# Fills of the third and fourth K stack behind a GpSimd copy of the second layer norm's result

## The chip, the cores and the metric

The kernel runs on one core of a Trainium2 chip. The core has five engines with a queue each: TensorE (PE, matrix products and transposes), VectorE (DVE), ScalarE (ACT), GpSimd (POOL) and SyncE (SP), which here issues every DMA. An engine works through its queue in order and waits at an instruction until the semaphores it needs have been raised by other engines. The metric is the time of one execution on the device in microseconds; shown is the median of several runs.

## The reference

The input `x` has 2048 rows of 512 in float32. The computation is one transformer block: a layer norm, an attention with memory, a residual, a second layer norm, a gated feed-forward part (GEGLU, 1376 wide) and a residual. Cut to what matters here:

```python
q, k, v = LN(x) @ wq, LN(x) @ wk, LN(x) @ wv      # 32 heads of 16, in 4 segments of 512 rows
for s in range(4):                                # M, z: a running memory per head
    p = softmax(q[s] @ k[s].T * 0.25 + causal_mask)
    o = g * (phi(q[s]) @ M) / (phi(q[s]) @ z + 1e-6) + (1 - g) * (p @ v[s])
    M, z = M + phi(k[s]).T @ v[s], z + sum(phi(k[s]))      # phi(t) = t + 1 or exp(t)
h = x + concat(o) @ wo
out = h + (gelu(LN(h) @ w_gate) * (LN(h) @ w_up)) @ w_down
```

## The kernel before

**Units and stages.** The 16 units of the attention are pairs of a chunk `c` (8 heads) and a segment `s`; the first is (0, 0), the second (0, 1). A unit has `qkv` (projections), `mem` (reading the memory), and for each of its two halves `Q` of four heads `pass_a` (row maxima of the logits) and `pass_b` (exponentials and the product with V). Then follow the output projection (`wo_seg`), the second layer norm of the block and the feed-forward part. Products are made of three float32r products of high and low parts, so most values exist as a rounded copy (made on ACT, as in L506) and a rest (made on DVE, as in L507, or on POOL, as in L394 and L410).

**The layer norms at the start.** `ln1(0)` and `ln1(1)` normalise the first and the second segment. For each, DVE takes statistics (L450, L451), works out the factors in twelve tiny steps (L455 to L466) and then normalises four tiles of 128x512 in place with four TENSOR_SCALAR instructions (L471). PE transposes them, four transposes for each of four column blocks `dc` (L497); ACT and DVE split every block into high and low parts (`xt`, L506 and L507). The transposes of `ln1(1)` write to PSUM banks of the pool `PD`, which has three banks and is shared with the projections: a bank is given back when its last reader is done, for example the two copies of a v projection's result on ACT (`vaug`, L576) or the DVE step of `phi` (L548). `ln1(2)` takes its statistics on ACT (L436, L445) with the two scratch tiles `junk`, which `pass_a` needs too (L711).

**The K stacks.** Four tiles `stk` hold K in the layout that `pass_a` and `pass_b` multiply with. DMAs write the K rows into them (L615); all else is constant and is filled once: by `c_stk(i, after)`, which for each half of the partitions issues one ACT copy of ones (64 partitions x 1024, L378) and one POOL memset of zeros (L381). So a stack has two ACT and two POOL instructions. Stacks 0 and 1 belong to the first unit, stacks 2 and 3 to the second.

**What sets the order.** No order is written by hand. The whole program is first listed as operations with an engine, a duration guessed in the code, a priority (a lower number goes first) and the values they read and write; `Sched.run` then deals them out greedily. At each step it takes, among the operations that could start within 0.059 us of the earliest possible start, the one with the lowest priority number. The guessed costs that matter here: a POOL copy of one column 0.1 us, the block of twelve small steps and four normalising steps of an early layer norm `3700 / 960 + 0.072` = 3.93 us, and from the end of an operation to the start of one that needs it 0.165 us (DVE to POOL), 0.08 (POOL to ACT), 0.27 (PE to ACT). Priorities: the splits of `ln1(1)` -2.21, the fills of stack 2 -2.2, those of stack 3 -1.2, the `vaug` copies of the first unit -1.58.

The order that comes out is the order of the engines' queues. The waits on the chip are set apart from it, from the tiles that instructions read and write. A value without a tile, such as those handed to `after`, orders the plan alone: nothing on the chip waits for it. That is why `ln1(0)` ends with a real instruction, a POOL copy of one column of its last normalised tile into `tick` (L523): the copy waits on the chip for the norm, and whatever stands behind it in POOL's queue waits with it. Its value `vcalm` orders the early fills behind it in the plan.

Of the kernel before, what the change touches and what calls it, by code (L numbers as in the profile page):

```python
# [212 lines left out]
def infini_geglu(ctx: ExitStack, tc: tile.TileContext, x, wq, wk, wv, wo, beta,  # L213
                 wg, wu, wd, out):
    nc = tc.nc
# [6 lines left out]
    def sb(name, shape, dt=F32):  # L222
        return p0.tile(shape, dt, name=name)
# [10 lines left out]
    def act(n, prio, fn, ins, outs, src=0.067, **k):  # L234
        return S.op("ACT", n / 1200 + src, prio, fn, ins, outs, **k)
# [4 lines left out]
    def pool(dur, prio, fn, ins, outs, **k):  # L240
        return S.op("POOL", dur, prio, fn, ins, outs, **k)

    def dma(prio, fn, ins, outs, lat=2.2, dur=0.58, **k):
        return S.op("SP", dur, prio, fn, ins, outs, lat=lat, **k)
# [61 lines left out]
    tick = sb("tick", [P, 1])  # L306
# [4 lines left out]
    vident, vamask, vmmask, vgt, vg1 = (Val() for _ in range(5))  # L311
# [31 lines left out]
                                base=0, channel_multiplier=1)  # L343
    pool(0.5, -9, c_ident, [], [vident])

    vcalm = Val()

# [1 line left out]
    vone, vq0, vk0, vv0 = Val(), [Val() for _ in stq_t], [Val() for _ in stk_t], [Val() for _ in va_t]  # L351
# [6 lines left out]
    def c_fill():  # L358
        for i, t in enumerate(stq_t):
            pool(0.93, -4.2 + 0.1 * i, lambda t=t: nc.gpsimd.memset(t.bitcast(F32), 0.0),  # L360
                 [vcalm] if i > 1 else [], [vq0[i]])
        for i, t in enumerate(va_t):
            def ones(t=t):
                nc.gpsimd.memset(t[:, :, 16:136:17], 1.0)
                nc.gpsimd.memset(t[:, :, 136:152], 1.0)
            pool(0.25, -3.5 + 0.1 * i, ones, [vcalm], [vv0[i]])

        def c_amask():
            nc.gpsimd.memset(amask, 0.0)
            nc.gpsimd.affine_select(amask[:, 3 * P:], amask[:, 3 * P:], pattern=[[-1, P]],  # L370
                                    compare_op=OP.is_ge, fill=NEG, base=0, channel_multiplier=1)
        pool(1.0, -3, c_amask, [vcalm], [vamask])

    def c_stk(i, after):
        t = stk_t[i]
        for a in range(2):
            own, other = slice(64 * a, 64 * a + 64), slice(64 - 64 * a, 128 - 64 * a)
            act(2 * D, -4.2 + i, lambda a=a, own=own: nc.scalar.activation(  # L378
                t[own, :, a], one[own, :, None].to_broadcast([64, 2, D]), AF.Copy),
                [vone] + after, [vk0[i]], src=0.1, chain=True)  # L380
            pool(0.93, -4.2 + i, lambda a=a, other=other: nc.gpsimd.memset(  # L381
                t[other, :, a].bitcast(F32), 0.0), after, [vk0[i]], chain=True)


    def split_weight(prio, src, pool_, w=D, rows=P, lo="POOL", after=(), early=3.0, dur=0.58):
        r = Val(PRAW)
        v = Val(pool_)
        dma(prio - early, lambda: nc.sync.dma_start(r.t[:rows, :w], src), [], [r], lat=3.0, dur=dur)
        act(w, prio, lambda: nc.scalar.activation(v.t[:rows, 0, :w], r.t[:rows, :w], AF.Copy),  # L389
            [r], [v], src=0.092)  # L390
        r.writers += [q for a in after for q in a.writers]
        sub = dict(op=OP.subtract)
        if lo == "POOL":
            pool(0.14 + 2.13e-3 * w, prio, lambda: nc.gpsimd.tensor_tensor(  # L394
                v.t[:rows, 1, :w], r.t[:rows, :w], v.t[:rows, 0, :w].bitcast(F32), **sub), [r], [v])
        else:
            dve(w, prio, lambda: nc.vector.tensor_tensor(
                v.t[:rows, 1, :w], r.t[:rows, :w], v.t[:rows, 0, :w].bitcast(F32), **sub), [r], [v])
        return v

    def split_wv(h, cp, prio, early, after=(), dur=0.58):
        hi, lo = WV[h, cp] = Val(PWV), Val(PWV)
        for k in range(2):
            r = Val(PRAW)
            dma(prio - early, lambda r=r, k=k: nc.sync.dma_start(
                r.t, wv[cp][:, k * D:(k + 1) * D]), [], [r], lat=3.0, dur=dur)
            act(D, prio, lambda r=r, k=k: nc.scalar.activation(hi.t[:, k], r.t, AF.Copy), [r], [hi],
                src=0.092, chain=True)
            r.writers += [q for a in after for q in a.writers]
            pool(1.23, prio, lambda r=r, k=k: nc.gpsimd.tensor_tensor(  # L410
                lo.t[:, k], r.t, hi.t[:, k].bitcast(F32), op=OP.subtract), [r, hi], [lo],
                chain=True)
# [99 lines left out]
    def ln1(s):  # L512
        prio = 2 * UNIT[0, s] + (-4.21)
        rows = [Val(PROW1 if s < 2 else PROW) for _ in range(4)]
        for t in range(4):
            r0 = (4 * s + t) * P
            dma(prio - 3, lambda t=t, r0=r0: nc.sync.dma_start(rows[t].t, x[r0:r0 + P]), [],
                [rows[t]], lat=2.0, dur=0.85 if s < 2 else 0.58)
        layer_norm(prio, rows, XT[s], off=s > 1, done=[Val()] if s < 2 else [],
                   behind=XT[0] if s == 1 else [], scratch=PPV if s < 2 else None)  # L520
        if s == 0:

            pool(0.1, prio, lambda: nc.gpsimd.tensor_copy(tick, rows[3].t[:, 0:1]), [rows[3]], [vcalm])  # L523


    va0 = list(vv0)
# [2 lines left out]
    W, STQ, STK, PQ, VA, MB, OM, MAXED = {}, {}, {}, {}, {}, {}, {}, {}  # L529
# [122 lines left out]
    def mem(U):  # L652
        c, s = UNITS[U]
        if not s:
            return
        prio = 2 * U + (-0.2)
        om = OM[U] = Val(POM)
        pq, mb = PQ[U], MB[UNIT[c, s - 1]]
        for n in range(2):
            pm, cc = Val(PD), Val(PCC)  # L660

            def f(n=n, pm=pm):
                for t in range(2):
                    nc.tensor.matmul(pm.t[:, 136 * t:136 * t + 136],  # L664
                                     pq.t[:, (2 * n + t) * P:(2 * n + t + 1) * P], mb.t,
                                     start=True, stop=True)
            pe(0.47, prio, f, [pq, mb], [pm], acq=[om, cc])

            def nd(pm):
                return pm.t[:, 0:272].rearrange("p (t j e) -> p t j e", t=2, j=8)  # L670
            dve(16, prio, lambda pm=pm, cc=cc, nd=nd: nc.vector.tensor_scalar(
                nd(pm)[:, :, :, 16], nd(pm)[:, :, :, 16], 1e-6, None, op0=OP.add), [], [pm])
            dve(128, prio, lambda pm=pm, nd=nd: nc.vector.reciprocal(
                nd(pm)[:, :, :, 16], nd(pm)[:, :, :, 16]), [], [pm])
            dve(16, prio, lambda pm=pm, cc=cc, nd=nd: nc.vector.tensor_tensor(
                cc.t, nd(pm)[:, :, :, 16],
                gt[:, None, 8 * c:8 * c + 8].to_broadcast([P, 2, 8]), op=OP.mult), [pm, vgt], [cc])

            def g(n=n, pm=pm, cc=cc, nd=nd):
                o4 = om.t.rearrange("p (t j e) -> p t j e", t=4, j=8)  # L680
                nc.vector.tensor_tensor(o4[:, 2 * n:2 * n + 2], nd(pm)[:, :, :, 0:16],
                                        cc.t[:, :, :, None].to_broadcast([P, 2, 8, 16]),
                                        op=OP.mult)
            dve(256, prio, g, [pm, cc], [om], chain=True)
# [247 lines left out]


    ln1(0)
    c_fill()
    for i in range(2):
        W[0, 0, i] = split_weight(-4 + 0.1 * i, (wq, wk)[i][0], PW, lo="DVE" if i == 0 else "POOL",
                               early=3.05, after=[vcalm], dur=0.85)
    split_wv(0, 0, -3.8, 2.5, [vcalm], 0.85)
    c_stk(0, [])  # L940
    c_stk(1, [vcalm])
    qkv(0)
    ln1(1)

    dma(1, lambda: nc.sync.dma_start(
# [11 lines left out]
    for U in range(16):  # L957
        c, s = UNITS[U]
        if U:
            qkv(U)  # L960
        if U == 0:
            c_stk(2, [VA[0]])
            c_stk(3, [VA[0]])
        if s % 2 and U < 15:
            h, cn = divmod(U // 2 + 1, NCH)
            for i in range(2):
                W[h, cn, i] = split_weight(2 * (U + 1) + (-3.175), (wq, wk)[i][cn], PW)
            if c % 2:
                split_wv(h, cn // 2, 2 * (U + 1) - 2.4, 3.0)
        if U in LN1_AT:  # L970
            ln1(LN1_AT[U])
        mem(U)
        pass_a(2 * U)
        if U:
            pass_b(2 * U - 1)
        pass_a(2 * U + 1)
        pass_b(2 * U)
# [7 lines left out]
    def at(p, f):  # L985
        return 40 + 24 * p + 2 * forder.index(f)
# [133 lines left out]
    for p in range(2):  # L1120
# [8 lines left out]
        for n, f in enumerate(forder):  # L1129
            k = 11 * p + n + 2  # L1130
            if k == 12:
                B[1] = blocks()
                for s in range(2):
                    prio = at(0, 8) + s
                    rows = [Val(PROW) for _ in range(4)]
# [53 lines left out]
```

## Time and profile before

| | |
|---|---|
| median of 3 runs | 850.38 us (849.77 to 851.44) |
| the profiled execution, its own time | 850.29 us |
| its span from first to last instruction | 848.2 us |
| PE busy | 825.0 us, 97% of the span |
| DVE, ACT, POOL busy | 621.8, 511.7, 458.7 us |
| mean granted PE clock | 0.998 of full speed |

A row of the timeline has the start in microseconds from the start of the span, the duration (of the whole group where equal instructions are merged: x4), the engine, the line of the kernel, the operation, the tile written and the tile read, and in brackets how long the engine had been idle and what ended that. SPq rows are DMA issues. In a table by windows, each row is a stretch of time with the busy time of every engine and the granted PE clock. The chain of waits goes back from the last instruction to what released it; its rows have a start, a length and what ran.

### The profile page before, as it was taken

The numbers are of one execution on the slowest core, as the hardware profiler recorded it, in microseconds if no ns is written. First come the engines' busy times: TensorE is split into PE (matmuls) and PEld (weight loads), VectorE is DVE, ScalarE is ACT, GpSimd is POOL, SyncE is SP. The second block draws the span as 40 slices with busy tenths as digits, with TensorE's granted clock in tenths as the row PEclk, the third lists the DMA queues.
The fourth block names the chain that finished last, engine by engine and source line by source line (L and its number), as shares of the span: only waits on it lengthen the run. The fifth ranks groups of instructions, "written<-read, shape, count | busy, mean of one in ns | idle before, by whom it ended". The sixth has DMA issues, their size and how long they took to land.

```text
span 848.2 us, 15681 instructions
## 1 busy us (share of the span) xinstructions
PE 825.0 (97%) x4924; PEld 656.3 (77%) x4924; DVE 621.8 (73%) x1963; ACT 511.7 (60%) x966; POOL 458.7 (54%) x791
## 2 busy tenths in 40 slices
PE   4899999999999999999999999999999999999998
PEld 4787777877788777887777688788888877788886
DVE  7788877779867778868698675565666885756656
ACT  6767667578755666557445763774656764636441
POOL 6433534434335453445333673588878767779650
PEclk9999999999999999999999999999999999999999
DMA  7444432444344333243343464422212351122102
GB/s 248 120 119 96 96 74 69 108 103 96 85 121 122 89 85 97 48 121 90 107 122 122 126 230 143 122 72 63 63 51 62 119 158 38 50 63 62 51 1 100
DMA packets 64179, 82.90 MB, mean 98 GB/s; under 512 B 25056, under 2 KB 27040, under 8 KB 64096
## 3 DMA queue, kind: packets, MB, share of 16 engines
q1 hardware_dynamic: 64096, 81.91, 34.8%
q8 instruction: 39, 0.64, 0.3%
q14 instruction: 44, 0.36, 0.2%
HBM read 43.14 MB, written 12.58 MB: 66 GB/s over the span
## 4 chain that ended last, share of the span: by engine, by line
PE 92%; DVE 4%; ACT 2%; issue 1%; DMA 1%; SPq 0%; POOL 0%; ACTq 0%; DVEq 0%; POOLq 0%
PE bank L1031 24%; PE bank L1092 14%; PE bank L536 10%; PE bank L701 9%; PE bank L756 9%; PE bank L785 8%; PE bank L862 5%; PE bank L565 4%; PE bank L497 2%; PE bank L808 2%; PE bank L664 1%; PE bank L640 1%; PE bank L632 1%; PE bank L855 1%; ACT pt L760 1%
## 5 line engine op out<-in xcount | busy, mean ns | idle before, releaser
L711 DVE CUSTOM_DVE_ANT_0 junk<-bank,amask 128x256 f32<-128x256 f32 (+3 forms) x512 | 231.0, 486 | 54.1 <-PE bank L701 49.8
L764 POOL TENSOR_SCALAR_AFFINE_SELECT pt<-pt 128x128 f32<-128x128 f32 (+1 forms) x448 | 131.8, 314 | 202.5 <-ACT pt L760 192.1
L760 ACT ACTIVATE pt<-bank 128x512 f32<-128x512 f32 x320 | 177.8, 602 | 63.0 <-PE bank L756 50.4
L701 PE MATMUL bank<-stk,stq 128*128 128x512 f32 (+2 forms) x384 | 130.5, 386 | 0.9 <-DVE nm L711 0.5
L756 PE MATMUL bank<-stq,stk 128*128 128x384 f32 (+3 forms) x512 | 119.8, 325 | 1.3 <-ACT pt L760 0.8
L536 PE MATMUL bank<-xt,w 128*128 128x512 f32 x384 | 109.2, 397 | 0.0
L756 PEld LDWEIGHTS bank<-stq,stk 128*128 128x128 f32 x512 | 85.8, 189 | 15.4 <-ACT pt L760 6.2
L1097 DVE TENSOR_TENSOR pt<-pt,bank 128x512 f32<-128x512 f32 x96 | 64.9, 685 | 28.7 <-PE bank L1092 28.3
L701 PEld LDWEIGHTS bank<-stk,stq 128*128 128x128 f32 x384 | 66.8, 189 | 19.5 <-issue 9.3
L536 PEld LDWEIGHTS bank<-xt,w 128*128 128x128 f32 x384 | 70.0, 189 | 10.9
L785 PE MATMUL bank<-pt,vaug 128*32 128x512 f32 (+3 forms) x1024 | 76.0, 436 | 0.0
L785 PEld LDWEIGHTS bank<-pt,vaug 128*32 128x32 f32 x1024 | 28.4, 109 | 39.9 <-issue 31.8
L1001 POOL TENSOR_TENSOR w<-raw,w 128x512 fp32r<-128x512 f32 (+2 forms) x36 | 42.4, 1180 | 25.4 <-ACT w L999 24.1
L394 POOL TENSOR_TENSOR w<-raw,w 128x512 fp32r<-128x512 f32 (+1 forms) x26 | 34.1, 1312 | 40.6 <-ACT w L389 24.0
L1031 PE MATMUL bank<-xt,stk 128*128 128x512 f32 (+1 forms) x189 | 53.0, 394 | 0.3 <-ACT pq L1038 0.3
L565 PE MATMUL bank<-wv,xt 128*128 128x256 f32 x384 | 52.7, 284 | 0.0
L565 PEld LDWEIGHTS bank<-wv,xt 128*128 128x128 f32 x384 | 50.6, 190 | 1.1
L1031 PE MATMUL bank<-xt,w 128*128 128x512 f32 (+1 forms) x183 | 50.8, 391 | 0.0
L1001 POOL TENSOR_TENSOR stk<-raw,stk 128x512 fp32r<-128x512 f32 (+3 forms) x32 | 36.9, 1155 | 20.1 <-ACT stk L999 19.7
L804 ACT ACTIVATE pvs<-bank 128x512 f32<-128x512 f32 x32 | 19.2, 598 | 44.9 <-PE bank L785 44.9
L1031 PE MATMUL bank<-stk,w 128*128 128x512 f32 (+1 forms) x162 | 45.5, 392 | 0.0
L711 DVE DVE_READ_ACCUMULATOR2_ANT nm<- 128x1 f32 x512 | 42.2, 82 | 0.0
(271 smaller groups left out, 1731.3 us busy)
## 6 DMA issues: line engine op xcount, KB each, us to landing
stq<-hl SPq DMA_DIRECT2D x96, 128.0 KB
stk<-hl SPq DMA_DIRECT2D x192, 64.0 KB
row<-x SPq DMA_DIRECT2D x24, 256.0 KB
raw<-wg SPq DMA_DIRECT2D x20, 256.0 KB
raw<-wu SPq DMA_DIRECT2D x20, 256.0 KB
raw<-wd SPq DMA_DIRECT2D x20, 256.0 KB
o_dram<-o SPq DMA_DIRECT2D x32, 128.0 KB
row<-o_dram SPq DMA_DIRECT2D x16, 256.0 KB
```

Source lines behind the costliest of these rows:

```text
L536: nc.tensor.matmul(pm.t, w.t[:, wi, dc * P:(dc + 1) * P], XT[s][dc].t[:, xi, :], start=dc == 0 and n == 0, stop=dc == ND - 1 and n == 2)
L565: nc.tensor.matmul(pm.t[:, 256 * t:256 * t + 256], XT[s][dc].t[:, xi, t0:t0 + P], whl[wi].t[:, h, 256 * (dc % 2):256 * (dc % 2) + 256], st ...
L701: nc.tensor.matmul(sa.t[:, k * w:(k + n) * w].rearrange("x (n w) -> x n w", n=n), sq.t[:, p, i * P:(i + 1) * P], sk.t[:, p, a:a + n, 0:w], ...
L711: nc.vector.tensor_tensor_reduce(out=junk.t[:, :w], in0=sa.t[:, k * w:(k + 1) * w], in1=amask[:, D - w:], op0=OP.add, op1=OP.min, scale=-1 ...
L756: nc.tensor.matmul(sc.t[:, lo:lo + D - q0], sk.t[:, p, a, q0:q0 + P], sq.t[:, p, q0:D], start=True, stop=True)
L760: act(D, prio, lambda: nc.scalar.activation(e.t, sc.t, AF.Exp), [sc], [e])
L764: nc.gpsimd.affine_select(v, v, pattern=pat + [[1, P]], compare_op=OP.is_ge, fill=0.0, base=0, channel_multiplier=-1)
L785: nc.tensor.matmul(pv.t[32 * n:32 * n + 32, kb * P:D], va.t[:, kb, 17 * j:17 * j + 32], e.t[:, lo:lo + D - kb * P], start=kb == 0, stop=la ...
L1001: pool(0.14 + 2.13e-3 * (hi - lo), prio, lambda: nc.gpsimd.tensor_tensor(v.t[:, 1, :hi - lo], r.t[:, lo:hi], v.t[:, 0, :hi - lo].bitcast(F ...
L1031: nc.tensor.matmul(dst.t[:w], v.t[:, wi, c0 + j * w:c0 + (j + 1) * w], b[bk][j].t[:, xi, :], start=first and j == 0 and n == 0, stop=j == ...
L1092: nc.tensor.matmul(pm.t, HH[p, f, s][hi].t[:w, t * P:(t + 1) * P], v.t[:w, wi, :], start=f == fl[0] and n == 0, stop=f == fl[-1] and n == 2)
L1097: dve(D, prio, lambda a=a, pm=pm: nc.vector.tensor_tensor(a.t, a.t, pm.t, op=OP.add), [pm], [a])
```

## The change

`ln1(1)` gets a POOL copy of one column of its last normalised tile too, and `vcalm` becomes a pair of values, one for each of the two layer norms. What hung on `vcalm` hangs on `vcalm[0]` now. The fills of stacks 2 and 3, which were ordered behind `VA[0]` (the `vaug` copies of the first unit), are ordered behind `vcalm[1]`, the new copy.

```diff
-    vcalm = Val()
+    vcalm = [Val(), Val()]
...
-                 [vcalm] if i > 1 else [], [vq0[i]])
+                 [vcalm[0]] if i > 1 else [], [vq0[i]])
...
-        if s == 0:
-
-            pool(0.1, prio, lambda: nc.gpsimd.tensor_copy(tick, rows[3].t[:, 0:1]), [rows[3]], [vcalm])
+        if s < 2:
+
+            pool(0.1, prio, lambda: nc.gpsimd.tensor_copy(tick, rows[3].t[:, 0:1]), [rows[3]],
+                 [vcalm[s]])
...
-    c_stk(1, [vcalm])
+    c_stk(1, [vcalm[0]])
...
         if U == 0:
-            c_stk(2, [VA[0]])
-            c_stk(3, [VA[0]])
+            c_stk(2, [vcalm[1]])
+            c_stk(3, [vcalm[1]])
```

The lines left out put `vcalm[0]` for `vcalm` in the same way, in the fills of `vaug`, in the mask and in the first weights.

More of the change, by code (lines that the diff above doesn't have):

```diff
@@ L365, in ones @@
                 nc.gpsimd.memset(t[:, :, 136:152], 1.0)
-            pool(0.25, -3.5 + 0.1 * i, ones, [vcalm], [vv0[i]])
+            pool(0.25, -3.5 + 0.1 * i, ones, [vcalm[0]], [vv0[i]])
         def c_amask():
@@ L371, in c_amask @@
                                     compare_op=OP.is_ge, fill=NEG, base=0, channel_multiplier=1)
-        pool(1.0, -3, c_amask, [vcalm], [vamask])
+        pool(1.0, -3, c_amask, [vcalm[0]], [vamask])
     def c_stk(i, after):
@@ L937, in infini_geglu @@
         W[0, 0, i] = split_weight(-4 + 0.1 * i, (wq, wk)[i][0], PW, lo="DVE" if i == 0 else "POOL",
-                               early=3.05, after=[vcalm], dur=0.85)
-    split_wv(0, 0, -3.8, 2.5, [vcalm], 0.85)
+                               early=3.05, after=[vcalm[0]], dur=0.85)
+    split_wv(0, 0, -3.8, 2.5, [vcalm[0]], 0.85)
     c_stk(0, [])
-    c_stk(1, [vcalm])
+    c_stk(1, [vcalm[0]])
     qkv(0)
```

## The prediction

> **What bounds the kernel now.** I read the page's totals and its chain first, then the table by windows, then the timeline of each engine around the second layer norm.
>
> ```profile
> span 848.2 us, 15681 instructions
> PE 825.0 (97%) x4924; PEld 656.3 (77%) x4924; DVE 621.8 (73%) x1963; ACT 511.7 (60%) x966; POOL 458.7 (54%) x791
> PE 92%; DVE 4%; ACT 2%; issue 1%; DMA 1%; SPq 0%; POOL 0%; ACTq 0%; DVEq 0%; POOLq 0%
> ```
>
> The chain of waits that ended last runs through PE for 92% of the span. So a change is worth what it takes out of PE's idle time. The windows from 40 us on say where idle time is left:
>
> ```profile
> 450.00:500.00 50.00, 47.13 (x299) 34.46 (x300) 39.09 (x114) 30.41 (x57) 28.62 (x54) 1.00 0.45 148
> 830.00:848.20 18.20, 14.41 (x64) 11.61 (x62) 10.97 (x17) 2.39 (x4) 0.00 (x0) 1.00 0.31 116
> sum 808.20, PE 798.22 PEld 634.00 DVE 591.90 ACT 484.01 POOL 436.60; mean PE 46.95 PEld 37.29 DVE 34.82 ACT 28.47 POOL 25.68
> ```
>
> Behind 40 us PE idles 808.20 - 798.22 = 10.0 us: 18.20 - 14.41 = 3.8 at the very end, 50 - 47.13 = 2.9 where attention passes into the rest of the block, 3.3 in all else. So a head start won before 40 us is kept to the end if the later order of work is as good as it is now. The change acts before 40 us, on DVE and POOL:
>
> ```profile
> 10.03 1.92 DVE L471 TENSOR_SCALAR pt<-pt,mv,ln 128x512 f32<-128x512 f32 x4
> 12.01 0.58 POOL L523 COPY tick<-pt 128x1 f32<-128x1 f32 x1 [5.29 <-DVE pt L471]
> 12.53 1.84 POOL L360 MEMSET stq<- 128x1024 f32 x2
> 13.14 0.69 DVE L507 TENSOR_TENSOR xt<-bank,xt 128x512 fp32r<-128x512 f32 x1 [0.60 <-ACT xt L506]
> 15.70 0.69 DVE L507 TENSOR_TENSOR xt<-bank,xt 128x512 fp32r<-128x512 f32 x1 [0.16 <-ACT xt L506]
> 17.52 0.95 POOL L381 MEMSET stk<- 64x1024 f32 x1
> 20.55 5.91 PE L565 MATMUL bank<-wv,xt 128*128 128x256 f32 x48
> 21.82 2.56 POOL L394 TENSOR_TENSOR w<-raw,w 128x512 fp32r<-128x512 f32 x2
> 22.48 0.15 DVE L455 TENSOR_SCALAR bank<-mv 128x4 f32<-128x4 f32 x1
> 24.44 4.45 POOL L381 MEMSET stk<- 64x1024 f32 x4
> 24.88 4.29 DVE L471 TENSOR_SCALAR pt<-pt,mv,ln 128x512 f32<-128x512 f32 x4
> 29.10 0.67 DVE L548 SCALAR_TENSOR_TENSOR pk<-bank,e 128x512 f32<-128x512 f32 x1
> ```
>
> The four normalising steps of the first norm take 1.92 us, the same four of the second 4.29. Beside the second run the four memsets of stacks 2 and 3: 4.45 us for four, 1.11 each, against 0.95 for one (17.52). Steps and memsets take turns, 4.29 / 4 = 1.07 for a step. So the fills had not waited for `VA[0]` at all; that value orders only the plan.
>
> [...]
>
> What the slow norm holds up:
>
> ```profile
> 28.07 0.33 PE L497 MATMUL bank<-ident,pt 128*128 128x128 f32 x1 [0.84 <-DVE pt L471]
> 29.23 2.56 PE L497 MATMUL bank<-ident,pt 128*128 128x128 f32 x9 [0.84 <-DVE pt L471]
> 29.00:30.00 1.00, 0.65 (x2) 0.36 (x3) 1.00 (x6) 0.26 (x1) 0.00 (x0) 0.50 0.67 156
> 31.00:32.00 1.00, 1.00 (x5) 0.93 (x4) 0.46 (x2) 0.74 (x2) 0.00 (x0) 0.50 0.42 102
> 27.05 1.05 ACT L378 ACTIVATE stk<-one 64x1024 fp32r<-64x1024 f32 x1
> 29.75 0.60 ACT L506 ACTIVATE xt<-bank 128x512 fp32r<-128x512 f32 x1 [1.65 <-PE bank L497]
> 30.98 0.60 ACT L506 ACTIVATE xt<-bank 128x512 fp32r<-128x512 f32 x1 [0.64 <-PE bank L497]
> 31.83 0.60 ACT L506 ACTIVATE xt<-bank 128x512 fp32r<-128x512 f32 x1 [0.26 <-PE bank L497]
> 32.46 1.05 ACT L378 ACTIVATE stk<-one 64x1024 fp32r<-64x1024 f32 x1
> 34.65 2.12 ACT L378 ACTIVATE stk<-one 64x1024 fp32r<-64x1024 f32 x2
> 36.80 0.72 ACT L445 ACTIVATE junk<-row,bn 128x512 f32<-128x512 f32 x1
> 37.76 0.69 DVE L711 CUSTOM_DVE_ANT_0 junk<-bank,amask 128x512 f32<-128x512 f32 x1 [1.48 <-ACT junk L445]
> 33.22 1.65 PE L536 MATMUL bank<-xt,w 128*128 128x512 f32 x6
> 38.51 0.50 PE L701 MATMUL bank<-stk,stq 128*128 128x512 f32 x1 [0.54 <-DVE nm L711]
> ```
>
> PE waits for single normalised tiles at 28.07 and 29.23, and its clock falls to 0.50 in the windows from 29 to 32. ACT waits three times for transposes, then does the rest without a pause: splits, the ACT part of the fills, L445. L445 gives back the scratch tile that DVE's first row maximum needs at 37.76, and PE goes on with `pass_a` at 38.51.
>
> **The change part by part.** *The memsets leave the norm.* The steps start at 24.88 as before, since nothing ahead of them is touched: the weight rests L394 end at 21.82 + 2.56 = 24.38. They take 1.92 instead of 4.29, so they end about 26.80 instead of 29.17: **2.37 us sooner**. DVE's L548 follows at once, and with it the PSUM bank for the next transposes.
>
> *What is late next.* It is ACT. From the fill at 27.05 to L445 its queue holds idle time of 1.65 + 0.64 + 0.26 = 2.55 us; more than that can't go, because the instructions stay the same. So DVE's first maximum and PE's restart at 38.51 come earlier by the lesser of 2.37 and 2.55. PE's products L536 of the second unit (33.22) move with the splits. The half clock brings nothing beyond that while ACT is the limit.
>
> *The copy and the moved memsets on POOL.* The copy costs 0.58 (12.01) and waits for the norm; the gap from 10.03 + 1.92 to 12.01 is 0.06. From 26.9 on: 0.58 + 4 x 0.95 = 4.4, so the fills end about 31.3 instead of 28.89.
>
> ```profile
> 40.70 1.31 POOL L394 TENSOR_TENSOR w<-raw,w 128x512 fp32r<-128x512 f32 x1 [11.80 <-ACT w L389]
> 43.70 3.73 SPq L615 DMA_DIRECT2D stk<-hl x6
> ```
>
> POOL stands idle for 11.80 us behind the fills, so nothing is queued behind the waiting copy before 40.70; even 2.4 us earlier that is 38.3. The first DMAs into stack 2 go out at 43.70. The cover is 7 us at POOL and 10 at the DMAs; without it each memset would cost its 0.95. No DMA is added, removed or moved past another on SP.
>
> *The ACT part of the fills* has no wait on the chip for the copy; only its place in the plan moves. The planner guesses 3.93 us for the block that starts at 22.48, which on these starts ends at 26.41; plus 0.165, 0.1 and 0.08 the fills are free at 26.76. The v projection ends at 20.55 + 5.91 = 26.46, plus 0.27 is 26.73 for its first `vaug` copy, and the second would follow about 0.3 later. So it is a near tie, and by priority (-2.2 against -1.58) the first ACT fill should overtake the second `vaug` copy, and two splits and the next fill with it: 1.05 + 2 x 0.5 + 1.05 = 3.1 us in which that copy holds a `PD` bank (0.5 is a split in a row without pauses, my estimate from the 0.60 of a single one). The third block's transposes then wait for the bank of the first split instead. Counting through with these durations, L536 starts about 31.5 instead of 33.22, 1.7 sooner, and PE's wait of 0.54 before 38.51 goes too: 2.2. With the old order it is 2.37, with all of ACT's idle time gone 2.55. I take **2.4**.
>
> *The rest of the plan.* Since starts in the plan shift by some tenths, the greedy dealing will pick differently in many places up to the end. No row prices that. Bounds: a gain of 2.9 if the idle time between 450 and 500 us went; a loss of 6.0 by the first rival below. I take 0, because in the long stretches PE is full (3.3 us idle beside the join and the end), and swapping work in a full queue costs nothing.
>
> Sum: 850.29 (profiled execution; its span of 848.2 and 2.1 around it) - 2.4 = 847.9. The median of the runs is 850.38, 0.1 from it.
>
> **The rivals.**
>
> *Slower: the join of attention and the rest runs dry.* There the last `pass_b` steps are a relay between engines, and PE is fed from other work.
>
> ```profile
> 458.41 0.61 ACT pt L760
> 460.04 0.99 PE bank L756 x3
> 473.07 0.41 ACT pvs L804
> 475.68 0.99 PE bank L756 x4
> 483.65 0.70 DVE vaug L891
> 488.23 0.63 PE bank L808 x4
> ```
>
> These rows of the chain bound three stretches in which the path is off PE: 1.6, 2.6 and 4.6 us, 8.8 in all; PE idles only 2.9 of these 50 us because transposes and `wo` products fill the rest. If the new order has spent that filler earlier, they stand bare: 8.8 - 2.9 = 5.9 more, 847.9 + 5.9 = **853.8**. It decides from 2.4 + 1.7 = 4.1 us on. For it: the order now wastes so little that another one is likelier to waste more than less. Against it: the same priorities deal it.
>
> *No change: the new order loses about what was won*, one more wait like the 2.10 us before L808 at the join (the windows' 2.9 holds it): 847.9 + 2.1 = **850.0**.
>
> *The half clock comes at a worse time.* PE still idles about a microsecond behind the v projection. If the clock falls to 0.50 for three windows under the dense products L536 and L701 instead of the transposes, that takes up to 3 x 0.5 = 1.5 us: **849.4**. Against it: less idle time. [...]
>
> *The change doesn't do what it says*: the plan puts other POOL work beside the norm. One weight rest, 2.56 / 2 = 1.28, would hold a step of 0.48 by 0.8, two by 1.6, leaving 0.8: **849.5**. Against it: the rests end half a microsecond before the steps, and nothing orders them anew.
>
> **How the numbers follow.** This measurement can tell about 0.2%, 1.7 us, from no change. Forecast kept: 0.42 (faster). Join dry: 0.40 (slower). New order loses what was won 0.10, half clock 0.05, other POOL work 0.03: together 0.18 (within 0.2%). The forecast's own range is 846.9 to 848.6. The range for 8 in 10 goes from 845.5 (half of the gain at the join, 2.9, and a little more on ACT) to 853.8.
>
> **What would show it.** In the changed trace: a second COPY of `tick` near 26.9, four memsets behind it at 0.95 to 31.3; L471 of the second norm at 1.92; ACT without pauses from 27 on; the first L711 near 35.3, PE's `pass_a` near 36.1, L394 near 38.3. Then PE's idle time behind 40 us against 10.0, above all in 450 to 500 against 2.9. Wrong would be: steps still at about 1 us each, a new idle stretch of PE between 27 and 36, or a gain at 38 us that is gone at 500.

## The result and the profile after

The changed kernel is slower: 853.67 us (median of 6, 853.17 to 854.06) against 850.84 before on the same chip, a ratio of 1.0033 with a 95% interval of 1.002 to 1.0046. Run again beside the experiments it came to 853.77 against 851.33, 1.0023 (1.0012 to 1.0035). The forecast was 847.9, a gain. The profiled execution took 853.52. A ratio in this text is the one on record with its interval; it is not always the quotient of the two medians beside it.

The page of the changed kernel:

```profile
span 851.9 us, 15688 instructions
PE 828.3 (97%) x4924; PEld 657.3 (77%) x4924; DVE 617.7 (73%) x1963; ACT 511.3 (60%) x966; POOL 457.1 (54%) x792
PE 87%; DVE 4%; ACT 3%; issue 2%; POOL 1%; DMA 1%; SPq 0%; DVEq 0%; ACTq 0%; POOLq 0%
```

PE does the same 4924 products, and the chain runs through it less often (87% for 92%). The timeline of the changed kernel around the second norm (lines behind 524 are one higher than before):

```profile
25.41 1.92 DVE L471 TENSOR_SCALAR pt<-pt,mv,ln 128x512 f32<-128x512 f32 x4
27.39 0.18 POOL L523 COPY tick<-pt 128x1 f32<-128x1 f32 x1 [3.04 <-DVE pt L471]
27.64 3.95 POOL L381 MEMSET stk<- 64x1024 f32 x4
27.31 1.04 ACT L378 ACTIVATE stk<-one 64x1024 fp32r<-64x1024 f32 x1
28.26 1.06 ACT L506 ACTIVATE xt<-bank 128x512 fp32r<-128x512 f32 x2
29.34 1.05 ACT L378 ACTIVATE stk<-one 64x1024 fp32r<-64x1024 f32 x1
30.40 0.38 ACT L577 ACTIVATE vaug<-bank 128x256 f32<-128x256 f32 x1
35.38 0.69 DVE L712 CUSTOM_DVE_ANT_0 junk<-bank,amask 128x512 f32<-128x512 f32 x1 [0.34 <-ACT junk L445]
36.13 0.50 PE L702 MATMUL bank<-stk,stq 128*128 128x512 f32 x1
```

Up to here the course is as forecast: the norm takes 1.92 us, the copy waits, the memsets follow it, a fill, two splits and a fill overtake the last `vaug` copy, and PE takes up `pass_a` at 36.13 instead of 38.51. The loss comes later. To find the place I compared how far PE had come: each product counts with its usual spacing in the kernel before, and for a time in that kernel the table says how much later (+) or earlier (-) another kernel had done the same amount of PE work.

```
time in the kernel before       24     40     52     56    180    480    500    840
changed                       +0.53  -1.74  -1.63  +0.30  +1.67  +1.99  +3.44  +3.58
changed, run again            +0.56  -1.72  -0.79  +1.13  +2.52  +2.88  +2.89  +2.90
```

The offset at 24 us lies ahead of everything that was changed. At 52 us the changed kernel leads by 1.63. Four us later 1.9 us are lost, and at 180 a further 1.4. That 1.4 is a net figure: up to about 170 us the two kernels do their work in different orders, and in between the lag goes up to 4.4 (at 110) and comes back to 1.6 (at 170). From 180 on the difference to the kernel before stays within 0.4 us for three hundred microseconds: the orders have met again. The 1.45 between 480 and 500 are not there when it is run again; see the half clock below. The place of the first loss, in the timeline of the changed kernel, PE first, then DVE:

```profile
49.34 0.63 PE L665 MATMUL bank<-mb,pq 128*128 128x136 f32 x4
49.71 0.48 PE L702 MATMUL bank<-stk,stq 128*128 128x512 f32 x1
50.40 0.51 PE L702 MATMUL bank<-stk,stq 128*128 128x512 f32 x1 [0.21 <-DVE nm L712]
51.10 0.44 PE L702 MATMUL bank<-stk,stq 128*128 128x384 f32 x1 [0.19 <-DVE nm L712]
51.71 0.94 PE L702 MATMUL bank<-stk,stq 128*128 128x384 f32 x2 [0.17 <-DVE nm L712]
52.48 0.27 PE L735 MATMUL bank<-ident,mm 128*32 128x128 f32 x1
52.88 0.97 PE L702 MATMUL bank<-stk,stq 128*128 128x384 f32 x2
53.70 0.86 PE L537 MATMUL bank<-xt,w 128*128 128x512 f32 x3
...
52.06 0.29 DVE L644 TENSOR_TENSOR mb<-bank,mmask 128x136 f32<-128x136 f32 x1
54.59 0.26 DVE L672 TENSOR_SCALAR bank<-bank 128x16 f32<-128x16 f32 x2
58.07 0.41 DVE L682 TENSOR_TENSOR om<-bank,cc 128x256 f32<-128x256 f32 x1
```

From 49.7 to 53.7 PE has, but for one short transpose (L735), only `pass_a` of the second half and goes at the pace of DVE's row maxima. In the kernel before, the projections of the third unit (there L536) lay between those products, and DVE's mask (there L643) came before them:

```profile
51.28 0.29 DVE L643 TENSOR_TENSOR mb<-bank,mmask 128x136 f32<-128x136 f32 x1
51.77 0.86 PE L536 MATMUL bank<-xt,w 128*128 128x512 f32 x3
52.47 0.39 PE L701 MATMUL bank<-stk,stq 128*128 128x512 f32 x1
52.70 0.86 PE L536 MATMUL bank<-xt,w 128*128 128x512 f32 x3
```

In the changed kernel they start at 53.70. They need a bank of `PD`, and in this order DVE's step that masks the second unit's memory update (L644) and its steps that read the memory (L672 to L682), which hold the three banks, stand behind the maxima. So the planner could deal the projections only late. The bank that L644 gives back at 52.06 + 0.29 = 52.35 goes first to the transpose of the maxima (L735 at 52.48), which DVE copies out here:

```profile
53.22 0.27 DVE L738 COPY mx<-bank 32x128 f32<-32x128 f32 x1
```

That ends at 53.49, and L537 follows at 53.70.

### The profile page after: what moved, and what is told of

Read it like the earlier page. It is cut to its first block, busy times and chain, and to the rows that moved or that the text cites. A ratio compares the mean times of both kernels' runs of the same rounds, so it can differ in the third digit from the quotient of the medians.

```text
span 851.9 us, 15688 instructions
## 1 busy us (share of the span) xinstructions
PE 828.3 (97%) x4924; PEld 657.3 (77%) x4924; DVE 617.7 (73%) x1963; ACT 511.3 (60%) x966; POOL 457.1 (54%) x792
## 4 chain that ended last, share of the span: by engine, by line
PE 87%; DVE 4%; ACT 3%; issue 2%; POOL 1%; DMA 1%; SPq 0%; DVEq 0%; ACTq 0%; POOLq 0%
PE bank L1032 23%; PE bank L1093 13%; PE bank L537 10%; PE bank L757 9%; PE bank L702 9%; PE bank L786 7%; PE bank L863 5%; PE bank L566 4%; PE bank L497 2%; PE bank L809 2%; DVE junk L712 1%; PE bank L665 1%; PE bank L641 1%; ACT pt L761 1%; PE bank L856 1%
## 5 line engine op out<-in xcount | busy, mean ns | idle before, releaser
L537 PE MATMUL bank<-xt,w 128*128 128x512 f32 x384 | 110.0, 399 | 0.6 <-DVE xt L507 0.6
L1098 DVE TENSOR_TENSOR pt<-pt,bank 128x512 f32<-128x512 f32 x96 | 65.0, 685 | 28.8 <-PE bank L1093 28.4
L537 PEld LDWEIGHTS bank<-xt,w 128*128 128x128 f32 x384 | 70.0, 190 | 11.6 <-DVE xt L507 0.8
L1032 PEld LDWEIGHTS bank<-xt,stk 128*128 128x128 f32 (+1 forms) x189 | 35.3, 190 | 8.9 <-ACT pq L1039 0.7
```

The lines of the kernel that those rows point to most:

```text
L537: nc.tensor.matmul(pm.t, w.t[:, wi, dc * P:(dc + 1) * P], XT[s][dc].t[:, xi, :], start=dc == 0 and n == 0, stop=dc == ND - 1 and n == 2)
L1032: nc.tensor.matmul(dst.t[:w], v.t[:, wi, c0 + j * w:c0 + (j + 1) * w], b[bk][j].t[:, xi, :], start=first and j == 0 and n == 0, stop=j == ...
L1098: dve(D, prio, lambda a=a, pm=pm: nc.vector.tensor_tensor(a.t, a.t, pm.t, op=OP.add), [pm], [a])
```

## The experiments

Two theories stood at the start. *Two separate terms*: the wait brings the 2.4 us of the forecast, and the new order takes more than that. *The rival*: a head start before 40 us is lost later whatever the order.

**order_kept: the wait without the new order.** The second copy is planned at 0.4 us instead of 0.1. Then the fills come free in the plan just behind the second `vaug` copy, and the queues are those of the kernel before with the copy alone added. (The same queues come out with the copy left at 0.1 and the `vaug` copies' priority put above the fills'.)

```diff
-            pool(0.1, prio, lambda: nc.gpsimd.tensor_copy(tick, rows[3].t[:, 0:1]), [rows[3]],
+            pool(0.4 if s else 0.1, prio, lambda: nc.gpsimd.tensor_copy(tick, rows[3].t[:, 0:1]), [rows[3]],
```

> The change with the second copy planned at 0.4 us instead of 0.1: the fills no longer overtake the second vaug copy in the plan, and the queues of all engines come out as in the kernel before, with the copy alone added on GpSimd. Theory (the wait is worth about 2.4 us, the new order costs 3.6 to 6): the norm's four steps take 1.9 us, PE's pass_a restarts near 36, the lead of 2 to 2.5 us is kept to the end, 848.0 to 848.6 against 850.4 to 850.8 before. Rival 1 (a head start before 40 us is lost later whatever the order, for example at the join by the half clock): 850 or more. Rival 2 (the copy itself does harm on GpSimd): above 851.

Measured: 849.88 us against 851.44, 0.9973 (0.9962 to 0.9984); once more on another occasion 849.23 against 850.49, 0.9982 (0.9973 to 0.999). Its timeline:

```profile
24.57 1.92 DVE L471 TENSOR_SCALAR pt<-pt,mv,ln 128x512 f32<-128x512 f32 x4
26.55 0.19 POOL L523 COPY tick<-pt 128x1 f32<-128x1 f32 x1 [1.97 <-DVE pt L471]
26.80 3.95 POOL L381 MEMSET stk<- 64x1024 f32 x4
35.30 0.50 PE L701 MATMUL bank<-stk,stq 128*128 128x512 f32 x1 [0.42 <-DVE nm L711]
36.11 0.23 ACT L947 ACTIVATE gt<-gt 128x32 f32<-128x32 f32 x1 [1.00 <-DMA gt<-beta]
48.84 0.47 PE L701 MATMUL bank<-stk,stq 128*128 128x512 f32 x1 [0.33 <-issue]
49.14 0.86 PE L536 MATMUL bank<-xt,w 128*128 128x512 f32 x3
49.84 0.39 PE L701 MATMUL bank<-stk,stq 128*128 128x512 f32 x1
50.06 0.84 PE L536 MATMUL bank<-xt,w 128*128 128x512 f32 x3
```

With the old order the wait is a gain, L536 alternates with `pass_a` from 49 on, and the lead holds from 52 to 480 us (table below). The times are above the 848.0 to 848.6 that the theory named. The medians differ by 1.6 and 1.3 us and the ratios say 2.3 and 1.5, where the theory said 2.4. Rival 2 falls. Rival 1 falls as a rule, since the time stays below that of the kernel before, but it has a part of the truth: in both profiled executions the half clock at the join takes 1.4 or 1.5 us of a lead of 2.3 or 2.4, so it is not kept to the end there.

**no_wait: the new order without the wait.** The copy reads a constant column.

```diff
-            pool(0.1, prio, lambda: nc.gpsimd.tensor_copy(tick, rows[3].t[:, 0:1]), [rows[3]],
+            pool(0.1, prio, lambda: nc.gpsimd.tensor_copy(tick, one if s else rows[3].t[:, 0:1]), [rows[3]],
```

> The changed kernel in its own order, but the second copy reads a constant column, so it waits for nothing and the four memsets run beside the norm again. Theory (the wait and the order are two separate terms): slower than the changed kernel by 1.5 to 2.5 us, 855 to 856, with steps of about 1.1 us in the second norm. Rival (in the new order the norm is not what PE waits for, so the wait brings nothing): 853.2 to 854.0, like the changed kernel.

Measured: 856.32 us, 1.0056 (1.0043 to 1.007). In its timeline the collision is back:

```profile
24.98 4.46 POOL L381 MEMSET stk<- 64x1024 f32 x4
24.99 4.73 DVE L471 TENSOR_SCALAR pt<-pt,mv,ln 128x512 f32<-128x512 f32 x4
```

By ratios the wait is worth 0.23% to 0.33% in the new order (against the two runs of the changed kernel), 2.0 to 2.8 us, and the order costs 0.41% to 0.60%, 3.5 to 5.1 us (the changed kernel's two ratios against order_kept's two). The two terms stand apart, as the theory says; the time is a little above the 855 to 856 expected.

**other_order_a and other_order_b: is any other order worse?** The first takes order_kept with another window of the planner, the second plans the copy at 0.9 us.

```diff
-    def run(self, window=0.059, stay=0.1):
+    def run(self, window=0.065, stay=0.1):
```

```diff
-            pool(0.1, prio, lambda: nc.gpsimd.tensor_copy(tick, rows[3].t[:, 0:1]), [rows[3]],
+            pool(0.9 if s else 0.1, prio, lambda: nc.gpsimd.tensor_copy(tick, rows[3].t[:, 0:1]), [rows[3]],
```

> The order_kept kernel with the planner's window of 0.059 set to 0.065: the same work and waits, the first third of PE's queue as before, the rest dealt otherwise. Theory (the order before is a lucky draw and nearly any other costs): 1 to 6 us above order_kept, so 849 to 854. Rival (the order of the changed kernel is an unlucky draw, others are as good as the one before): within 1 us of order_kept.

> The change with the second copy planned at 0.9 us: the fills are planned a little later still, and the order becomes a third one, neither that of before nor that of the changed kernel. Theory (lucky draw): 1 to 6 us above order_kept, 849 to 854. Rival (only the fill that overtakes the vaug copy and holds a PSUM bank costs, and that doesn't happen here): within 1 us of order_kept.

Measured: 849.4 and 849.5 us, both 0.9975 (0.9964 and 0.9965 to 0.9985), as fast as order_kept. For these two orders the theory of the lucky draw falls: the changed kernel's order has something bad in it that they lack. They do not weigh the same. PE's queue in other_order_a is that of order_kept for its first 997 of 4924 products, up to about 156 us (a fifth, not the third that was expected), so it tests the later order alone; only other_order_b deals the early part anew.

**mask_first and mask_mem_first: the held banks.** The changed kernel, with the priority of one DVE step of the second unit altered, the mask L643. The second kernel also moves the DVE steps that read the memory.

```diff
-        dve(136, prio + 0.8, lambda: nc.vector.tensor_tensor(
+        dve(136, prio + 0.8 if U != 1 else -1.5, lambda: nc.vector.tensor_tensor(
```

```diff
-        prio = 2 * U + (-0.2)
+        prio = 2 * U + (-0.2); dp = prio if U != 1 else -1.5
...
-            dve(16, prio, lambda pm=pm, cc=cc, nd=nd: nc.vector.tensor_scalar(
+            dve(16, dp, lambda pm=pm, cc=cc, nd=nd: nc.vector.tensor_scalar(
...
```

> The changed kernel as it is, once more, so that the edits to it below are compared on one chip. All theories: about 1.0033 of the kernel before (1.002 to 1.0046), some 854 if before stands at 851.4.

> The changed kernel with one priority altered: the VectorE step that masks the second unit's memory update (L643) is dealt ahead of the row maxima of pass_a, so it gives its PSUM bank back before the projections of the third unit are due. Theory (in the new order that step and the reads of the memory stand behind the row maxima on VectorE, all three banks of the pool are held, and PE runs pass_a alone at VectorE's pace from 49 to 54 us): the projection L536 starts near 50 instead of 53.7, and the time falls by 1.5 to 4 us below the changed kernel, to 0.998 to 1.0015 of before. Rival (the order loses in many small places, the stretch at 49 us is only where it shows): within 1 us of the changed kernel.

> As mask_first, and the VectorE steps of reading the second unit's memory (L671 to L681) are dealt ahead of the row maxima too, so the other two banks come back early as well. Theory (held banks): at least as fast as mask_first, 0.997 to 1.000 of before. Rival (many small places): within 1 us of the changed kernel.

Measured, all on one chip: the changed kernel 853.77 (1.0023), mask_first 849.17 (0.9963, interval 0.9951 to 0.9975), mask_mem_first 850.23 (0.9985, 0.9972 to 0.9998). The timeline of mask_first, DVE's mask and PE's stretch:

```profile
49.21 0.29 DVE L643 TENSOR_TENSOR mb<-bank,mmask 128x136 f32<-128x136 f32 x1
...
49.45 0.48 PE L701 MATMUL bank<-stk,stq 128*128 128x512 f32 x1
49.77 0.84 PE L536 MATMUL bank<-xt,w 128*128 128x512 f32 x3
50.45 0.39 PE L701 MATMUL bank<-stk,stq 128*128 128x512 f32 x1
50.68 0.86 PE L536 MATMUL bank<-xt,w 128*128 128x512 f32 x3
```

The mask runs at 49.21 instead of 52.06, the projection at 49.77 instead of 53.70, and the lead at 56 us is 2.12 instead of a lag of 0.30. With one DVE step of 0.29 us dealt earlier the loss turns into a gain, 4.6 us where at most 4 were expected. But the altered priority also deals the rest anew, so not all of that is this one bank: 2.4 us of it are there at 56 us and the rest comes later. mask_mem_first was expected to be at least as fast as mask_first and is not. Its mask runs at 49.29, its reads of the memory are done at 52.73 instead of 57.06, and it loses nothing between 52 and 56 us either; but by 180 us its lead has gone from 1.98 to 0.73, while mask_first still has 2.03. So the stretch at 49 us is shown to be the first part of the loss, by held banks; where the net 1.4 us between 56 and 180 go was not taken apart.

**act_fills_late: is ACT the limit before 40 us?** Order_kept, with the ACT part of the fills at a low priority.

```diff
-            act(2 * D, -4.2 + i, lambda a=a, own=own: nc.scalar.activation(
+            act(2 * D, -4.2 + i if i < 2 else 12, lambda a=a, own=own: nc.scalar.activation(
```

> The order_kept kernel with the ACT part of the fills of stacks 2 and 3 at the priority of the third layer norm's statistics (12 instead of -2.2 and -1.2): 4.2 us of fills no longer stand ahead of L445, which gives VectorE its scratch tile. Theory (from 27 us on ACT is what PE waits for): the first row maximum comes 1 to 2 us before that of order_kept (35 us), PE restarts earlier, and the time is 0.5 to 2 us below order_kept, 0.995 to 0.997 of before. Rival (PE is then short of work it may start, since the projections wait for the splits and banks): the same as order_kept, 0.997 to 0.998.

Measured: 850.6 us, 0.9985 (0.997 to 0.9999), above what either side expected, though the interval reaches down to it. The local part of the theory holds, and by more than the 1 to 2 us expected: DVE's first row maximum starts here at 31.58, in order_kept at 34.55; the next, at 34.98, waits for `junk`. The first two rows are of this kernel, the last is of order_kept:

```profile
31.58 0.68 DVE L711 CUSTOM_DVE_ANT_0 junk<-bank,amask 128x512 f32<-128x512 f32 x1
34.98 0.69 DVE L711 CUSTOM_DVE_ANT_0 junk<-bank,amask 128x512 f32<-128x512 f32 x1 [0.79 <-ACT junk L445]
34.55 0.69 DVE L711 CUSTOM_DVE_ANT_0 junk<-bank,amask 128x512 f32<-128x512 f32 x1 [1.33 <-ACT junk L445]
```

Counted from 24 us on, the lead at 44 is 3.5 us against 2.3 in order_kept. But the theory as a whole does not hold: this order too loses later, 2.3 us between 180 and 480. So the changed kernel's order is not the only one that costs time.

**beta_early: what is late next.** In order_kept ACT stands 1.00 us for the load of `beta` (row at 36.11). That DMA is issued behind the 18 DMAs into the stacks, which the wait does not move. Here it is issued behind an earlier weight load; the other queues stay. The planned operation remains in its place, empty:

```diff
-    dma(1, lambda: nc.sync.dma_start(
-        gt, bass.AP(tensor=beta.tensor, offset=beta.offset, ap=[[0, P], [1, 32]])), XT[1], [vgt])
+    dma(1, lambda: None, XT[1], [vgt])
...
-        dma(prio - early, lambda: nc.sync.dma_start(r.t[:rows, :w], src), [], [r], lat=3.0, dur=dur)
+        dma(prio - early, lambda: [nc.sync.dma_start(r.t[:rows, :w], src), also and also()], [], [r], lat=3.0, dur=dur)
```

> The order_kept kernel with one DMA moved on SP: the load of beta is issued behind the load of the first weight of the next chunk, near 16 us, instead of behind the 18 DMAs into the stacks, near 33 us. All queues but SP's are the same. Theory (with the wait in place the load of beta, which did not move, is what is late next: ACT stands 1.00 us for it at 36 us): that pause is gone, and PE's lead over the kernel before at 44 us grows by 0.4 to 0.7 us; the time falls by about as much below order_kept, 0.9965 to 0.9975 of before. Rival (something else comes due at the same moment): lead and time like order_kept.

> order_kept once more, beside beta_early on one chip: 0.9962 to 0.9984 of before by its earlier interval.

Measured: 848.46 us against 850.49, 0.9969 (0.9957 to 0.9981), beside 849.23 of order_kept. The pause is gone, as its timeline shows:

```profile
36.94 0.21 ACT L947 ACTIVATE gt<-gt 128x32 f32<-128x32 f32 x1
```

Counted from 24 us on, the lead at 44 is 2.87 for 2.30 in both runs of order_kept: 0.57, inside the 0.4 to 0.7 expected. The intervals of the two times overlap, so the gain in time is not shown by itself. Of the kernels that were run this one and mask_first have the lowest ratios; both beat the kernel before and the changed one.

PE's lead in all of them, less the offset at 24 us, from the traces as above:

```
time in the kernel before      40     44     52     56    180    480    500    840
changed                      -2.27  -2.09  -2.16  -0.23  +1.14  +1.46  +2.91  +3.05
changed, run again           -2.28  -1.28  -1.35  +0.57  +1.96  +2.32  +2.33  +2.35
no_wait                      +0.94  +1.12  +1.05  +4.51  +6.15  +6.31  +6.31  +6.33
order_kept                   -2.88  -2.30  -2.32  -2.36  -2.34  -2.26  -0.88  -0.16
order_kept, run again        -2.89  -2.30  -2.29  -2.32  -2.35  -2.38  -0.92  -0.87
beta_early                   -2.88  -2.87  -2.87  -2.90  -2.59  -2.61  -2.61  -2.63
other_order_a                -2.89  -2.45  -2.46  -2.47  -2.38  -2.05  -0.57  -0.13
other_order_b                -3.73  -3.32  -3.61  -3.58  -2.42  -2.51  -2.51  -2.49
mask_first                   -2.28  -2.09  -2.51  -2.39  -2.30  -2.11  -0.65  -0.71
mask_mem_first               -2.28  -1.44  -2.00  -1.99  -0.74  -0.64  -0.69  -0.59
act_fills_late               -3.66  -3.46  -3.59  -3.29  -2.82  -0.50  -0.51  -0.52
```

## Why the prediction was wrong

**Right.** *The memsets leave the norm*: 1.92 us, measured 1.92; putting the memsets back (no_wait) brings 4.73. *What is late next, ACT*: no pause from 27.31 to the first L445; the first maximum at 35.38 for 35.3, PE's `pass_a` at 36.13 for 36.1, in an execution that was 0.53 late at 24 us, so the gain at that point was rather 2.9 than 2.4. In order_kept too it is 2.9 (35.30 for 38.51, in an execution 0.31 early). That is more than the 2.55 of ACT's idle time that "can't go" beyond: from the first fill to L445 ACT takes 6.85 us in order_kept (26.74 to 33.59) for 9.75 before, in part because splits in a row take 0.51 us each for 0.60. *The near tie*: the two fills and two splits overtook the `vaug` copy as counted through. *The copy and the memsets on POOL* are hidden; the second copy takes 0.18 us, not the 0.58 of the first.

**Wrong: "The rest of the plan ... I take 0".** The term's range, -2.9 to +6.0, held what it cost, but the value was the wrong one. Against order_kept, the same wait in the old order, the new order costs 0.41% to 0.60%, 3.5 to 5.1 us; that is more than the wait brings. The reason given, that PE is full in the long stretches and swapping work in a full queue costs nothing, failed at its first word: between 49 and 54 us PE's queue held nothing but work paced by DVE, because three banks were held by DVE steps behind the row maxima and the planner dealt the projections behind those. A queue that was full in one order needn't be in another.

**Wrong place in the rival that came true in size.** It said 853.8 by a dry join at 450 to 500 us. There the changed kernel idles 50 - 46.70 = 3.3 us for 2.9:

```profile
450.00:500.00 50.00, 46.70 (x291) 33.89 (x291) 38.88 (x120) 29.97 (x57) 27.67 (x56) 0.97 0.48 153
```

The order's loss lies at 52 to 170 us, where none of my rows had been looked at for what feeds PE. That the rival's 853.8 agrees with the 853.67 measured is an accident.

**Too coarse: PE's idle time as the measure.** I named it as what would show the loss. Behind 40 us it is 811.9 - 800.5 = 11.4 us in the changed kernel (828.3 busy in all, less the 27.8 ahead of 40 us) for 10.0 before, 1.4 more, while 5.3 us of lead are lost (-1.74 to +3.58), 1.45 of them by the half clock at the join. Much of what is lost counts as busy. In the slow stretch PE is busy for 3.21 of 3.99 us:

```profile
49.71:53.70 3.99, 3.21 (x12) 1.52 (x11) 3.99 (x17) 0.00 (x0) 0.47 (x2) 1.00 0.61 162
```

But the products that start in it are worth 1.65 us by their usual spacing in the kernel before. So 2.3 us are lost where the idle time shows 0.8.

**The half clock at a worse time** (0.05) came in the profiled execution, though not where the rival put it, under L536 and L701, but at the join:

```profile
490.00:492.00 2.00, 1.79 (x8) 1.62 (x9) 2.00 (x6) 0.60 (x1) 2.00 (x3) 0.73 1.04 395
492.00:494.00 2.00, 2.00 (x6) 1.54 (x6) 2.00 (x6) 0.69 (x2) 1.84 (x3) 0.50 0.99 320
```

It costs 1.45 us there, but order_kept has it too (1.38 lost between 480 and 500 us), and the changed kernel run again does not (mean granted clock 1.000, 0.01 lost). So it comes and goes with the execution and is not shown to belong to the change. Only the half clock at 29 us goes with the slow norm: it is in the traces of the kernel before (0.50 in the windows from 29 to 32) and of no_wait (0.85 from 26 to 30, 0.50 from 30 to 34), and in none of the ten others. Of these, five have a mean granted clock of 1.000; the other five have 0.998 and lose 1.38 to 1.48 us between 480 and 500. That less idle time speaks against the half clock was my estimate from one place, the waits at 28.07 and 29.23 beside the 0.50 from 29 on; no run tested it.

**Missing.** The load of `beta` did not move with the rest and took back 0.57 us of the lead; I had checked SP for what passes what, not for what stays behind while its reader moves up. With that the gain of the wait is 2.9 at 40 us and 2.3 from 44 to 480. The line that no DMA is moved past another on SP was wrong for the changed kernel as well: there the load of `beta` goes out behind a weight load that it preceded before (two rows of the kernel before, then two of the changed one).

```profile
33.12 0.46 SPq L945 DMA_DIRECT2D gt<-beta  x1
33.67 0.38 SPq L405 DMA_DIRECT2D raw<-wv  x1
33.56 0.40 SPq L405 DMA_DIRECT2D raw<-wv  x1
34.02 0.42 SPq L946 DMA_DIRECT2D gt<-beta  x1
```

In the two traces of the changed kernel ACT stands 0.54 and 1.43 us for it, where the kernel before has no such wait.

## What to carry to other kernels

Where a planner deals the order, an edit has two prices: what it does on the chip, and what the changed guesses do to everything dealt after it; hold the order fixed (here by one guessed duration) to measure the first alone, and treat the second as unknown in sign and as large as the first. A new order is to be read at the places where a small pool of banks is given back by an engine that has a long queue of something else: there one short step in the wrong place stops another engine. And when a wait is taken out, list what its beneficiaries will need earlier that does not move with them.

## What the runs showed of the hardware

The half clock lasted 3.41 us in the kernel before (28.97 to 32.39) and 3.41 in the changed kernel (490.92 to 494.33); the one behind the last product is left out. In no_wait the windows give about 6.8 us from about 28.8 on (granted clock 0.85 from 26 to 30, 0.50 from 30 to 34, 0.80 from 34 to 38), and another one from about 56.1 (0.76 from 54 to 58). By the clock records of the two traces it started 13.65 us after the clock first rose to full in the kernel before and 474.45 us after that in the changed one, which are 4 and 139 times 3.413. The first rise itself lies at 15.32 us in the kernel before and at 16.47 in the changed one. The 24 projections that run across it (L536, there L537) took 6.03 and 6.57 us, and at 24 us the changed kernel stands 0.53 late. PE was not idle throughout in the 3.41 us just ahead of a low stretch: it was busy for 1.89 of them ahead of the one at 28.97 in the kernel before (25.56 to 28.97) and for 1.30 ahead of the one at 490.92 in the changed kernel (487.51 to 490.92). Around the one near 56.1 in no_wait it was busy for 3.62 of the 4 us from 50 to 54 and 3.62 from 54 to 58. What sets the moment was not shown. Whether the join is hit differs from one execution of a kernel to the next: of the two traces of the changed kernel one has it. Of 12 executions of order_kept, the 5 with a mean granted clock of 1.000 took 847.99 to 849.21 us, the 7 with 0.998 took 849.83 to 850.69. In the same session 10 of 27 executions of the kernel before had 0.996 or less (851.81 to 853.92 us), and none of order_kept.

DVE's normalising steps and POOL's memsets started by turns in the kernel before: memsets at 24.44, 25.44, 26.61 and 27.78, steps at 24.88, 25.59, 26.76 and 27.93, from the second on 1.17 us apart. With both started together (no_wait) four steps took 4.73 us, 1.18 each, beside memsets of 1.12, where alone they take 0.48 and 0.99 (order_kept). Their times overlap: one after the other four of each would take 1.92 + 3.95 = 5.87 us, and side by side they were done in 4.74 (24.98 to 29.72). DVE's splits L507 took no longer beside memsets: in the changed kernel 0.69 and 0.68 us at 28.86 and 29.47, with the memsets from 27.64 to 31.58, and 0.69 at 32.87 without one.
